# Branch prefetch hints on four engines, the fp64 weights decoded in the expert units, their clamp on GpSimd

## The chip, the cores and the metric

The kernel runs on one core of a Trainium2 chip. The metric is the device time in microseconds (us) of one execution; several executions are timed, and their median counts. One further execution is recorded by the hardware profiler, and all rows below come from that one. Engines: PE = TensorE, DVE = VectorE, ACT = ScalarE, POOL = GpSimd, SP = SyncE (it issues most DMAs).

## The reference

Three layers follow one another on 2304 tokens with 512 channels, in float32; the weights of the third are given as float64.

```
x = decayed_causal_attention(q, k, v, f)        # 4 x 8 heads, 576 tokens, 64 wide
e = argmax(x @ w_gate + bias[modality])          # 8 experts, top 1
x = p[e] * (relu(x @ w1[e]) @ w2[e])             # 512 -> 1024 -> 512
gate = sigmoid(x @ moe2_w_gate)                  # 512 -> 1536, float64 weights
out = (gate * (x @ moe2_w_val)) @ moe2_w_out     # 1536 -> 512, float64 weights
```

## The kernel before

The program has three stages, one behind the other.

**Attention and routing** take the first 240 us or so. The routing sorts the tokens by expert.

**Expert units** (class `Experts`). A unit is 256 sorted tokens of one expert (units 0 to 8, `NA` = 9, method `pair`) or 128 (units 9 and up, `single`). Units 0 and 1 run beside the attention; units 2 to 8 stand behind it and take 23.46 us each, in eight steps f = 0 to 7. In a step PE multiplies the tokens with a block of w1 (`up`, L1208, 12 matmuls of 128x256) and the step before's activations with a block of w2 (`down`, L1218, 6 matmuls of 128x512). Each float32 operand is split in a high and a low part, so each product is three matmuls: ACT makes the high parts (weights L1125, activations L1178), DVE the low ones (weights `wl` L1131, activations `hl` L1179, tokens `xl` L1165). At the end of each step `extra(u, f)` adds work of the next stage. POOL issues the indirect DMAs that gather a unit's tokens (L1081) and scatter its results (L1188). Units 9 and 10 always run. Units 11 to 17 stand in nested `tc.If(nb > u - NA)` (L1802), where `nb` is read from the routing; with these inputs the first test skips all of them, so each engine takes one branch over the code of seven units.

**Gated layer** (class `Gated`). Three sets of 768 tokens, s = 0 to 2, are multiplied with gate, value (L1543) and output weights (L1631). The chip has no float64, so the float64 weights are turned into float32 on the way: they arrive as pairs of 32-bit words in 36 pieces of 512 KB (`load`, into three buffers `raw`), and `decode` makes a float32 piece of each with integer operations: ACT takes the absolute value of the high words (L1395), DVE clamps it (L1376), shifts it left by three and masks it (L1377), then merges in sign and top bit (L1386) and the upper bits of the low word (L1387). Two finished pieces are written to DRAM (`wd`, L1382) and read back as `wf` and `wof`.

`decode((0,))` issues the clamp and the shift. `decode((1,))` issues, in this order, the DMA of a finished pair, L1386 and L1387 of the piece under work, ACT's L1395 of the next piece and the DMA of a later one. A piece's load is thus issued two calls of `decode((1,))` before ACT reads it, and it waits until L1387 has freed its buffer. Before, `extra` calls one half in every step of units 2 to 8, so four pieces per unit; `AHEAD` = 28 pieces are meant for the expert units, and the last 8, with what is in flight, are decoded in the first set of the gated layer. The trace shows 25 pieces finished by DVE before 454.5 us and 11 after it. Each engine works through its instructions in the order of the program.

Of the kernel before, what the change touches and what calls it, by code (L numbers as in the profile page):

```python
# [10 lines left out]
F32 = mybir.dt.float32  # L11
# [4 lines left out]
ALU = mybir.AluOpType  # L16
# [17 lines left out]
NA = NT // 256  # L34
# [1288 lines left out]
class Gated:  # L1323
# [8 lines left out]
    NB, NH = 768, 384  # L1332
    NP, NS = FF2 // 256, NT // 768

    DIRECT, AHEAD = 4, 28

    STEPS = (0, 0), (1, 1), (4, 2), (3, 3), (5, 4), (6, 5), (2, 6)

# [30 lines left out]
    def decode(self, halves=(0, 1)):  # L1369

        nc = self.nc
        if self.c and 0 in halves:
            o, r = self.c[0][:2]
            nc.vector.tensor_scalar(o.bitcast(F32), o.bitcast(F32), MINH, MAXH, ALU.max, ALU.min)  # L1376
            nc.vector.tensor_scalar(o, o, 3, 0x3FFFFFF8, ALU.logical_shift_left, ALU.bitwise_and)  # L1377
        if 1 not in halves:
            return
        if self.done:  # L1380
            key, t = self.done.popleft()
            nc.sync.dma_start(self.wd[key], t.bitcast(F32))  # L1382
        if self.c:
            o, r, key, part = self.c.popleft()
            hw, lw = r[:, :, 1], r[:, :, 0]
            nc.vector.scalar_tensor_tensor(o, hw, -0x40000000, o, ALU.bitwise_and, ALU.bitwise_or)  # L1386
            nc.vector.scalar_tensor_tensor(o, lw, 29, o, ALU.logical_shift_right, ALU.bitwise_or)  # L1387
            if part:
                self.done.append((key, self.dec.pop(key)))
        if self.r and (len(self.r) > 1 or not self.todo):  # L1390
            key, part, r = self.r.popleft()
            if key not in self.dec:
                self.dec[key] = self.bp.tile([P, 2, 512], I32, tag="dec", name="dec", bufs=3)
            o = self.dec[key][:, part, :]
            nc.scalar.activation(o.bitcast(F32), r[:, :, 1].bitcast(F32), AF.Abs)  # L1395
            self.c.append((o, r, key, part))
        if self.todo:
            key, part = self.todo.popleft()
            self.r.append((key, part, self.load(key, part)))
# [331 lines left out]
MINH = float(_np0.array([0x38000000], dtype=_np0.uint32).view(_np0.float32)[0])  # L1731
MAXH = float(_np0.array([0x47EFFFFF], dtype=_np0.uint32).view(_np0.float32)[0])


@with_exitstack
def decayed_attention_top1_moe_gated_kernel(
    ctx: ExitStack,
    tc: tile.TileContext,
    q, k, v, f, moe_modality_id, moe_w_gate, moe_modality_bias, moe_w1, moe_w2,
    moe2_w_gate, moe2_w_val, moe2_w_out, out,  # L1740
):
    nc = tc.nc
    keep = ctx.enter_context(tc.tile_pool(name="keep", bufs=1))
    dram = ctx.enter_context(tc.tile_pool(name="dram", bufs=1, space=DRAM))
    xd = dram.tile([NT, DX], F32, tag="xd", name="xd")
    yd = nc.dram_tensor("rows_by_expert", [NT, DX], F32, kind="Internal").ap()
    ident = keep.tile([P, P], F32, tag="ident", name="ident")
    make_identity(nc, ident)

    c2 = ExitStack()  # L1750
    ps = Banks(c2.enter_context(tc.tile_pool(name="ps", bufs=1, space=PSUM)))
    raw = c2.enter_context(tc.tile_pool(name="ex_r", bufs=1))
    with ExitStack() as c1:
        ro = Routing(tc, c1, keep, xd, ident, moe_modality_id, moe_w_gate, moe_modality_bias)
        ex = Experts(tc, ro, ps, raw, xd, yd, moe_w1, moe_w2)
        ex.g[0], ex.g[1] = ro.xg[0:2], ro.xg[2:4]
        with ExitStack() as c0:
            with ExitStack() as top:
                with tc.manual_schedule():
                    att = Attention(tc, c0, top, ro, ps, q, k, v, f)  # L1760
                    ex.begin(att)
                    att.run(ex)
            ro_t = c1.enter_context(tc.tile_pool(name="ro_t", bufs=1, side="right", reuse_waits="tile"))
            with tc.manual_schedule():
                ex.tail(ro.finish(ro_t, ps), c1.enter_context(tc.tile_pool(name="ex_s", bufs=1, side="right", reuse_waits="tile")))
        sp = c2.enter_context(tc.tile_pool(name="sp", bufs=2, reuse_waits="tile"))
        ex.open(c2, sp)
        ctx.enter_context(tc.manual_schedule())
        ex.rest()

    bits = ctx.enter_context(tc.tile_pool(name="bits", bufs=1, side="right", reuse_waits="tile"))
    ga = Gated(tc, ro, bits, dram, ps, yd, moe2_w_gate, moe2_w_val, moe2_w_out, out)
    none = lambda u, f: None
    with c2:

        pace, todo = (1, 1, 1, 1, 1, 1, 1, 1), deque((0, 1) * (len(ga.todo) + 3))
        turns, first = deque((n, c) for n in range(2) for c in range(KD)), deque()

        def extra(u, f):
            if u < NA:  # L1780
                for _ in range(min(pace[f], len(todo))):
                    ga.decode((todo.popleft(),))

            if u == NA - 2 and f == 4:
                ga.rows(0)
            if u == NA - 1 and f == 4:
                ga.tokens(0)
            if u == NA - 1 and f >= 4 or u >= NA and f in (0, 4):
                ga.early(*turns.popleft())
            if u == NA + 1 and f == 0:  # L1790
                ga.fetch(0)
            if u == NA + 1 and f == 3:
                first.extend(f for _, f in ga.prepare(0))
            if u == NA + 1 and f == 5:
                ga.fetch(1)
            if u == NA + 1 and f >= 5:
                for _ in range(min(2, len(first))):
                    first.popleft()()

        ex.run(range(2, NA + 2), NA + 1, extra)  # L1800
        nb = nc.values_load(ro.tl[0:1, 2 * NU:2 * NU + 1], min_val=0, max_val=NB)
        with ExitStack() as ifs:  # L1802
            for u in range(NA + 2, NU):
                ifs.enter_context(tc.If(nb > u - NA))
                ex.start(u)
                ex.run([u], u, none)

    with ExitStack() as c3:
        ga.run(c3)
# [33 lines left out]
```

## Time and profile before

| what | us |
|---|---|
| timed runs | 905.07, 905.3, 906.23 (median 905.3) |
| profiled execution | 906.16 |
| its span, first to last instruction | 904.2 |
| PE busy | 871.4 (96%) |
| DVE busy | 691.4 (76%) |
| ACT busy | 547.4 (61%) |
| POOL busy | 233.1 (26%) |

All times of rows are counted from the span's start. The expert units end at 454.5 us, the gated layer begins at 458.0 us. A "busy" share is a mean over stages: between 300 and 420 us DVE is at 93%, at the end of the program far below that.

### The profile page before, as it was taken

To read this page: it belongs to the slowest core of one execution; us is meant where nothing else is said; L and a number is where in the kernel's file an instruction comes from. 1 tells how busy PE (TensorE), PEld (TensorE's weight loads), DVE (VectorE), ACT (ScalarE), POOL (GpSimd) and SP (SyncE) were. 2 spreads that over 40 slices of the span, in tenths; PEclk is the share of its full clock that TensorE was granted. 3 is DMA by queue.
4 is the path that set the end of the run, shared out by engine and by line. 5 is a ranking of instruction groups with operands and counts; after the bars stand their busy time and mean duration, and the time that the engine had idled before them with its cause. 6 is when DMAs were issued, how large, how long until landed. Compare 5 with 4: busy or idle time off the path is not lost. (4 is left out here: it accounts for less than half of the span.)

```text
span 904.2 us, 16679 instructions
## 1 busy us (share of the span) xinstructions
PE 871.4 (96%) x5563; PEld 757.2 (84%) x5563; DVE 691.4 (76%) x1665; ACT 547.4 (61%) x1179; POOL 233.1 (26%) x483
## 2 busy tenths in 40 slices
PE   8998999979999999999989899999999999999996
PEld 6776777758989999999779888999988999999995
DVE  7677788848888999999767886887665888766652
ACT  7776777754456666667834545566555567545442
POOL 5787777674542222111000000002000001100002
PEclk9999999999999999999989999999999999999999
DMA  6555666786535955589766423244221212312201
GB/s 147 131 124 140 173 162 147 217 211 162 100 106 166 331 180 178 184 240 341 254 236 191 140 70 94 71 141 140 70 71 51 89 61 96 104 67 70 70 1 70
DMA packets 121133, 126.54 MB, mean 140 GB/s; under 512 B 68208, under 2 KB 95344, under 8 KB 121040
## 3 DMA queue, kind: packets, MB, share of 16 engines
q1 hardware_dynamic: 115744, 110.48, 42.6%
q0 software_dynamic: 4640, 14.70, 4.8%
q8 instruction: 46, 0.75, 0.4%
q14 instruction: 47, 0.39, 0.1%
q10 hardware_dynamic: 656, 0.22, 0.1%
HBM read 126.78 MB, written 24.28 MB: 167 GB/s over the span
## 5 line engine op out<-in xcount | busy, mean ns | idle before, releaser
L1543 PE MATMUL g<-x,wc 128*128 128x384 f32 x1536 | 304.4, 340 | 10.6 <-PEq L1802 3.5
L1543 PEld LDWEIGHTS g<-x,wc 128*128 128x128 f32 x1536 | 275.9, 189 | 31.0 <-ACT pc L1580 4.4
L1631 PE MATMUL o<-wo,ah 128*128 128x512 f32 x648 | 184.5, 397 | 0.2 <-DVE ah L1568 0.2
L1631 PEld LDWEIGHTS o<-wo,ah 128*128 128x128 f32 x648 | 118.0, 188 | 11.7 <-DVE ah L1568 1.0
L1639 POOL DMA_INDIRECT out_dram<-os,tok x18 | 18.4, 1020 | 423.7 <-ACT os L1638 418.2
L1567 ACT ACTIVATE ah<-s 128x384 fp32r<-128x384 f32 x72 | 37.9, 526 | 99.9 <-DVE s L1566 96.6
L1131 DVE TENSOR_TENSOR wl<-ws,wh 128x1024 fp32r<-128x1024 f32 x76 | 92.3, 1217 | 1.0 <-ACT wh L1125 1.0
L1125 ACT ACTIVATE wh<-ws 128x1024 fp32r<-128x1024 f32 x76 | 80.4, 1062 | 15.6 <-PE y L1218 15.6
L293 POOL TENSOR_SCALAR dec<-cum 128x192 f32<-128x192 f32 (+4 forms) x150 | 79.9, 539 | 25.6 <-DMA cum<-drow 16.5
L360 ACT ACTIVATE sc<-sc,mn 128x192 f32<-128x192 f32 (+2 forms) x144 | 82.3, 573 | 2.9 <-DVE mn L352 2.4
L352 DVE CUSTOM_DVE_ANT_0 sc<-s,dec 128x192 f32<-128x192 f32 (+2 forms) x144 | 58.7, 441 | 22.5 <-POOL dec L293 8.7
L1208 PE MATMUL h<-xh,wh 128*128 128x256 f32 x240 | 69.0, 288 | 0.0
L1208 PE MATMUL h<-xl,wh 128*128 128x256 f32 x240 | 67.7, 282 | 0.0
L1208 PE MATMUL h<-xh,wl 128*128 128x256 f32 x240 | 67.7, 282 | 0.0
L1580 ACT ACTIVATE pc<-g 128x384 f32<-128x384 f32 x96 | 46.3, 483 | 31.1 <-PE g L1543 30.6
L1188 POOL DMA_INDIRECT rows_by_expert<-ys,dst x18 | 22.1, 1229 | 159.0 <-ACT ys L1187 56.4
L345 PE MATMUL s<-qk,qT 64*128 64x320 f32 (+4 forms) x384 | 55.7, 407 | 3.7 <-DVE mn L352 2.2
L1426 DVE TENSOR_TENSOR wc<-wf,wc 128x512 fp32r<-128x512 f32 x72 | 40.7, 568 | 18.2 <-ACT wc L1423 18.2
L1559 ACT ACTIVATE sg<-sg 128x384 f32<-128x384 f32 x48 | 25.2, 525 | 45.3 <-DVE sg L1589 18.8
L345 PEld LDWEIGHTS s<-qk,qT 64*128 64x128 f32 (+1 forms) x384 | 31.2, 177 | 23.6 <-issue 16.3
L1218 PE MATMUL y<-wh,hh 128*128 128x512 f32 x120 | 47.6, 397 | 0.7 <-ACT hh L1178 0.7
L1218 PE MATMUL y<-wh,hl 128*128 128x512 f32 x120 | 47.3, 394 | 0.6 <-DVE hl L1179 0.6
(306 smaller groups left out, 1809.5 us busy)
## 6 DMA issues: line engine op xcount, KB each, us to landing
ws<-in_moe_w_dram SPq DMA_DIRECT2D x88, 512.0 KB
wf<-wd SPq DMA_DIRECT2D x36, 512.0 KB
wd<-dec SPq DMA_DIRECT2D x18, 512.0 KB
wof<-wd SPq DMA_DIRECT2D x18, 512.0 KB
cum<-drow SPq DMA_DIRECT2D x30, 288.0 KB
raw<-in_moe_w_gate_dram SPq DMA_DIRECT2D x12, 512.0 KB
raw<-in_moe_w_val_dram SPq DMA_DIRECT2D x12, 512.0 KB
raw<-in_moe_w_out_dram SPq DMA_DIRECT2D x12, 512.0 KB
```

The costliest lines, as they stand in the source:

```text
L293: nc.gpsimd.tensor_scalar(d[r, o], c[r, z], -1.0, c[r, a:a + 1], ALU.mult, ALU.add)
L345: nc.tensor.matmul(out[r, o:o + w], q[a, rows], k[a, c:c + w], start=True, stop=True)
L352: nc.vector.tensor_tensor_reduce(s[:, so + c0:so + e], t[j, b, c0][:, 0:e - c0], d[:, do + c0:do + e], -1.0, mn[j][:, 5:6] if c0 else 3.0e ...
L360: nc.scalar.activation(so, so, AF.Exp, bias=mn[j][:, b:b + 1], scale=-1.0, accum_out=sm[:, c:c + 1])
L1125: self.nc.scalar.activation(hi, self.ws[k], AF.Copy)
L1131: eng.tensor_tensor(lo, self.ws[k], hi.bitcast(F32), ALU.subtract)
L1208: nc.tensor.matmul(t, a[:, c, cs], self.chunk(b, c), start=(n == 0), stop=(n == 3 * KD - 1))
L1218: nc.tensor.matmul(y[j], a[:, cs], b[:, f % 2, :], start=(f == 0 and n == 0), stop=(f == nf - 1 and n == 2))
L1426: V(t["w"][:, 1, to], of(), t["w"][:, 0, to].bitcast(F32), ALU.subtract)
L1543: self.nc.tensor.matmul(t, p[:, c, :], q[:, c, :], start=(first and n == 0), stop=(n == total - 1), skip_group_check=not first)
L1580: nc.scalar.activation(c, t, AF.Copy)
L1631: nc.tensor.matmul(o[0], x[:, cs], y[:, r, :], start=(o[1] == 0 and k == 0), stop=(o[1] == 2 * self.NP - 1 and k == 2))
```

## The change

`AHEAD` becomes 36: every piece is decoded in the expert units. The clamp goes from DVE to POOL (same operation and tile), the shift moves to the other half, ahead of the two merges. The one-half-per-step pace is replaced by a table of steps per unit, `slots`: in each of them the second half of one piece and the first half of the next are issued. That is five pieces in each of units 3 to 8, two in unit 9 and one in unit 10; all 36 loads are issued by the end of unit 8. A branch hint, "likely taken", is set for PE, ACT, DVE and SP on the first of the nested tests; POOL has none.

```diff
-    DIRECT, AHEAD = 4, 28
+    DIRECT, AHEAD = 4, 36
...
         if self.c and 0 in halves:
             o, r = self.c[0][:2]
-            nc.vector.tensor_scalar(o.bitcast(F32), o.bitcast(F32), MINH, MAXH, ALU.max, ALU.min)
-            nc.vector.tensor_scalar(o, o, 3, 0x3FFFFFF8, ALU.logical_shift_left, ALU.bitwise_and)
+            nc.gpsimd.tensor_scalar(o.bitcast(F32), o.bitcast(F32), MINH, MAXH, ALU.max, ALU.min)
...
             hw, lw = r[:, :, 1], r[:, :, 0]
+            nc.vector.tensor_scalar(o, o, 3, 0x3FFFFFF8, ALU.logical_shift_left, ALU.bitwise_and)
             nc.vector.scalar_tensor_tensor(o, hw, -0x40000000, o, ALU.bitwise_and, ALU.bitwise_or)
...
-        pace, todo = (1, 1, 1, 1, 1, 1, 1, 1), deque((0, 1) * (len(ga.todo) + 3))
+        slots = {2: (2, 3, 5, 6, 7), **dict.fromkeys(range(3, NA), (0, 2, 3, 6, 7)), NA: (1, 4), NA + 1: (1,)}
...
-            if u < NA:
-                for _ in range(min(pace[f], len(todo))):
-                    ga.decode((todo.popleft(),))
+            if (u, f) == (2, 0):
+                ga.decode((1,))
+                ga.decode((1,))
+            if f in slots.get(u, ()):
+                ga.decode((1,))
+                ga.decode((0,))
...
             if u == NA + 1 and f == 0:
+                tc.mark_branch_hint_location("more", "LikelyTaken", [e.engine for e in (nc.tensor, nc.scalar, nc.vector, nc.sync)])
                 ga.fetch(0)
...
-                ifs.enter_context(tc.If(nb > u - NA))
+                ifs.enter_context(tc.If(nb > u - NA, label="more" if u == NA + 2 else None))
```

Four lines are added above the branch, so L1802 of before is L1806 of the change; L1376 is the clamp in both; the shift L1377 is L1385 of the change, and L1386 and L1387 keep their numbers.

In the built program the hint stands not beside the branch but at the start. PE, start of the program:

```order
-L1838 UNCONDITIONAL_BRANCH
+L1842 UNCONDITIONAL_BRANCH
+L1842 BRANCH_PREFETCH_HINT
 L132 MATMUL t<-x 128x128 x10
```

The branch that it speaks of comes some 1,880 lines of this listing later; ACT, DVE and SP have it at the same place.

DVE, one stretch of steps in the middle of the expert units. `hl` and `wl` are the low parts that PE needs in the next steps, `dec` is a piece under work, `raw` its float64 words. Before:

```order
L1179 SCALAR_TENSOR_TENSOR hl<-h,hh 128x256
L1131 TENSOR_TENSOR wl<-ws_104,wh 128x1024
L1376 TENSOR_SCALAR dec<-dec 128x512
L1377 TENSOR_SCALAR dec<-dec 128x512
L1179 SCALAR_TENSOR_TENSOR hl<-h,hh 128x256
L1131 TENSOR_TENSOR wl<-ws_105,wh 128x1024
L1386 SCALAR_TENSOR_TENSOR dec<-raw,dec 128x512
L1387 SCALAR_TENSOR_TENSOR dec<-raw,dec 128x512
```

and with the change:

```order
L1179 SCALAR_TENSOR_TENSOR hl<-h,hh 128x256
L1131 TENSOR_TENSOR wl<-ws_104,wh 128x1024
L1385 TENSOR_SCALAR dec<-dec 128x512
L1386 SCALAR_TENSOR_TENSOR dec<-raw,dec 128x512
L1387 SCALAR_TENSOR_TENSOR dec<-raw,dec 128x512
L1179 SCALAR_TENSOR_TENSOR hl<-h,hh 128x256
L1131 TENSOR_TENSOR wl<-ws_105,wh 128x1024
L1179 SCALAR_TENSOR_TENSOR hl<-h,hh 128x256
```

The clamp has left DVE; the three operations of a piece stand in one block, and five steps of eight have one.

POOL, the same units. Before it had only indirect DMAs:

```order
L1081 DMA xg<-xd,ids 128x513 x2
L1188 DMA rows_by_expert<-ys,dst 2304x513 x2
L1081 DMA xg<-xd,ids 128x513 x2
L1188 DMA rows_by_expert<-ys,dst 2304x513 x2
L1081 DMA xg<-xd,ids 128x513 x2
```

and with the change:

```order
L1376 TENSOR_SCALAR dec<-dec 128x512 x3
L1081 DMA xg<-xd,ids 128x513 x2
L1376 TENSOR_SCALAR dec<-dec 128x512 x2
L1188 DMA rows_by_expert<-ys,dst 2304x513 x2
L1376 TENSOR_SCALAR dec<-dec 128x512 x3
```

Three clamps now stand ahead of each unit's gather, and two ahead of its scatter.

## Rows read from the trace of the kernel before

**Rows 1.** Stretches of time, us: length, busy time (instructions), PE clock, DMA share, GB/s.
```profile
core 0: us, PE busy (x) PEld busy (x) DVE busy (x) ACT busy (x) POOL busy (x), PEclk, DMA share, GB/s
...
325.00:350.00 25.00, 25.00 (x162) 22.54 (x161) 23.24 (x43) 16.54 (x26) 5.22 (x4) 1.00 0.53 170
...
400.00:420.00 20.00, 20.00 (x134) 18.16 (x134) 18.60 (x39) 13.80 (x24) 4.22 (x3) 1.00 0.95 312
...
440.00:454.50 14.50, 13.97 (x87) 11.48 (x86) 11.29 (x17) 10.53 (x20) 1.22 (x1) 1.00 0.40 152
454.50:458.00 3.50, 0.02 (x1) 0.00 (x0) 2.28 (x5) 0.69 (x1) 0.97 (x1) 0.77 0.12 36
458.00:462.00 4.00, 3.96 (x12) 3.99 (x13) 0.00 (x0) 0.00 (x0) 0.00 (x0) 0.50 0.64 154
...
500.00:520.00 20.00, 17.69 (x93) 15.77 (x93) 17.45 (x38) 11.24 (x24) 0.00 (x0) 1.00 0.51 158
520.00:540.00 20.00, 18.25 (x97) 16.26 (x96) 16.46 (x39) 9.58 (x21) 0.00 (x0) 1.00 0.27 79
540.00:560.00 20.00, 18.23 (x100) 16.29 (x99) 13.29 (x29) 10.35 (x23) 0.00 (x0) 1.00 0.35 106
...
650.00:700.00 50.00, 48.82 (x263) 44.61 (x262) 31.15 (x69) 26.82 (x56) 0.00 (x0) 1.00 0.18 53
```

**Rows 2.** Waits of the gated layer: engine, line, releaser: us, times, longest.
```profile
PE g L1543 <- PEq L1802: 3.5, 1, 3.5
```

**Rows 3.** Line 1802, the branch, by engine queue: duration in ns, start in us.
```profile
L1802 PEldq COMPARE_BRANCH  x1: 3792/3792/3792, 453.9 to 453.9; - x1
...
L1802 ACTq COMPARE_BRANCH  x1: 54/54/54, 455.1 to 455.1; - x1
...
L1802 ACTq EVENT_SEMAPHORE  x1: 17/17/17, 458.0 to 458.0; - x1
```

**Rows 4.** Chain that ended last: start us, us, what.
```profile
458.04 8.88 PE g L1543 x36
...
481.48 2.09 PE g L1543 x12
```

**Rows 5.** Stretches of time, instructions on tile `dec` alone: DVE, ACT, POOL.
```profile
277.00:454.50 177.50, 55.65 (x100) 17.47 (x26) 0.00 (x0) 1.00 0.70 231
454.50:560.00 105.50, 24.48 (x44) 6.66 (x10) 0.00 (x0) 0.97 0.50 157
```

**Rows 6.** Tile `dec`, DVE's operations on a piece: ns min/median/max.
```profile
L1376 DVE TENSOR_SCALAR dec<-dec x36: 416/421/428, 279.9 to 537.7; 128x512 f32<-128x512 f32 x36
L1377 DVE TENSOR_SCALAR dec<-dec x36: 426/428/429, 280.4 to 538.2; 128x512 int32<-128x512 int32 x36
L1386 DVE SCALAR_TENSOR_TENSOR dec<-raw,dec x36: 681/686/693, 282.8 to 538.6; 128x512 int32<-128x512 int32 x36
L1387 DVE SCALAR_TENSOR_TENSOR dec<-raw,dec x36: 691/692/695, 283.5 to 539.4; 128x512 int32<-128x512 int32 x36
```

**Rows 7.** Timeline of POOL, the scatter of two units: start us, us, what.
```profile
332.30 1.01 POOL L1188 DMA_INDIRECT rows_by_expert<-ys,dst  x1 [17.33 <-DVE ys L1186]
...
355.76 1.02 POOL L1188 DMA_INDIRECT rows_by_expert<-ys,dst  x1 [17.33 <-DVE ys L1186]
```

**Rows 8.** Groups of POOL by form: busy us, mean ns | idle before.
```profile
L293 POOL TENSOR_SCALAR dec<-cum 128x576 f32<-128x576 f32 x30 | 22.0, 745 | 0.0
L293 POOL TENSOR_SCALAR dec<-cum 128x448 f32<-128x448 f32 x30 | 19.0, 643 | 1.5
```

**Rows 9.** Timelines of POOL and DVE, routing: start us, us, what.
```profile
209.69 2.39 POOL L1131 TENSOR_TENSOR spare<-ws,spare 128x1024 fp32r<-128x1024 f32 x1
...
210.41 1.70 DVE L420 TENSOR_SCALAR r<-sm 128x9 f32<-128x9 f32 x1
```

**Rows 10.** One raw piece, its load on SP and ACT's reading; landing of the gathers.
```profile
408.03 0.38 SPq L1361 DMA_DIRECT2D raw<-in_moe_w_gate_dram  x1
...
418.03 0.69 ACT L1395 ACTIVATE dec<-raw 128x512 f32<-128x512 f32 x1 [0.82 <-DMA raw<-in_moe_w_gate_dram]
...
DMA to landing us min/median/max: 4.4/5.9/7.2
```

## The prediction

> **What bounds the kernel now.** I read the stretches of time first, since the busy shares of the whole program hide which engine limits which stage. In the expert units PE is busy without a gap and DVE nearly so: 23.24 us of 25.00, 93%, while ACT has a third of its time free and POOL four fifths [rows 1]. PE sets the pace there and DVE stands just under it. The second thing to see is the seam at 454.5 us: for 3.50 us PE does nothing, and in the four microseconds behind it PE's granted clock is 0.50, the lower of its two levels [rows 1]. The waits name the releaser: PE's own sequencer, at the branch of L1802, 3.5 us [rows 2]; the branch itself took 3792 ns on PE from 453.9 us, and ACT, whose branch took 54 ns at 455.1, has its next event at 458.0 [rows 3]. The chain that ended last starts there too: its first 36 matmuls took 8.88 us, while 12 at full clock take 2.09 [rows 4]. Third, behind 500 us PE loses 2.31, 1.75 and 1.77 us in three stretches of 20 us, against 1.18 in 50 us later on [rows 1]; the first two of them still hold decoding, of which 24.48 us on DVE and 6.66 us on ACT lie behind the branch [rows 5].
>
> **The change, part by part.**
>
> *Branch hint.* If it does what its name says, PE finds its code behind the branch ready. PE's idle time of 3.5 us [rows 2] would go, but for some 0.2 us for the branch itself (54 ns on ACT) and the semaphores beside it [rows 3]: about 3.3. With no pause the clock need not fall either: 36 matmuls at the full pace of rows 4 take 3 x 2.09 = 6.27, so 8.88 - 6.27 = 2.6 us come back. Sum -5.9. Bounds: 0 if the hint does nothing, -6.1 if nothing at all is left; what is late next is ACT, whose branch and events end at 458.0 [rows 3] and which has a hint too. I take -5.9, being nearer the row that shows the whole wait at one instruction. The hint instruction itself stands at the start of the program; I bound it by 0 and the 0.05 us of ACT's branch [rows 3] and take 0.
>
> *Gated layer.* It no longer decodes 11 pieces. PE's idle time between 500 and 560 us is 2.31 + 1.75 + 1.77 = 5.83 us. At the later rate (1.18 in 50, so 0.47 in 20) the first two stretches would give 4.06 - 0.94 = 3.1 us. The third has no decoding after 539.4 [rows 6] and loses as much as the second, so part of the idle time is not DVE's decoding but something else, perhaps weights read back late; of it I count 0.4. I take -3.5; bounds 0 (it is all something else) and -5.8 (all goes).
>
> *Expert units 3 to 8, DVE.* A unit lasts 355.76 - 332.30 = 23.46 us [rows 7]; DVE is busy 0.93 x 23.46 = 21.8 and idle 1.64. Four pieces cost 4 x (421 + 428 + 686 + 692) ns = 8.91 us; five without their clamp cost 5 x 1.806 = 9.03 [rows 6]. That alone is +0.12 and harmless. The clamp on POOL is not shown; between 448 and 576 columns POOL's tensor_scalar takes 643 to 745 ns [rows 8], so some 0.69 us for 512. POOL has room for five of them. The doubt is whether DVE stands still meanwhile. One place shows that it can: POOL's L1131 ran from 209.69 to 212.08, and a tiny DVE operation of 9 columns, begun at 210.41, ended at 212.11, 0.03 us behind it [rows 9]. So each clamp may hold DVE for anything between 0 and 0.69 us. Some of it lies beside DVE work that is not held or beside a wait, so I take 0.45. Then DVE needs 21.8 + 0.12 + 5 x 0.45 = 24.2 us in a unit of 23.46: 0.75 too much, and over six units +4.5 us, since PE can then only wait for `hl` and `wl`. Bounds: 0 (clamps in DVE's idle time) to 6 x (0.12 + 5 x 0.69 - 1.64) = +11.6.
>
> The Trainium skill ("SBUF — State Buffer", section "SBUF: two separate sides") speaks against this move: DVE and GpSimd share a pair of ports, and the one that starts first holds it for its whole instruction while the other is blocked. Rows 9 agree with it in that one place. By that rule a clamp that has started would hold back the merges and `wl`, and the sum would go towards the upper bound; a clamp that arrives during them would wait at no cost to DVE.
>
> *Raw loads.* A load is issued when L1387 frees its buffer, and read by ACT two calls later. Before, that is always four steps, 11.73 us, of which 10.00 - 0.82 = 9.2 were left in the case of rows 10. With the table of steps the distance is two steps from f = 6 to the next f = 0 (3.3 us left), three from 0 to 3 and from 7 to 2 (6.2 left), four otherwise. Landing takes 4.4 to 7.2 us for the gathers, which are half as large, and 10 us for a raw piece where the DMA engines are 95% busy [rows 1, 10]. So ACT will wait 1 to 4 us in every unit, 2 or so of which its third of free time takes, and more where expert weights are loaded as well. Bounds 0 and +8 (two such units of the six, one wait of 3.8 us each unhidden, doubled); I take +1.0, nearer 0, since ACT waited only 0.82 us in the fullest stretch so far. POOL's gathers stand behind three clamps now, that is some three steps (9 us) later, but a unit ahead of their use; the scatter's two clamps are short. Both I price at nothing: a whole unit of 23.46 us covers them.
>
> *Units 9 and 10.* They decode three pieces more, 5.4 us on DVE. DVE has 14.50 - 11.29 = 3.2 us free in 440 to 454.5, and PE loses 0.53 there already [rows 1]. I take +1.0; bounds 0 and +3.
>
> Sum: -5.9 - 3.5 + 4.5 + 1.0 + 1.0 = -2.9. The profiled execution took 906.16 us (its span 904.2 and 1.96 around it), so it would take 903.3. It lies 0.86 above the median of the timed runs, 905.3, and against the median the forecast is **902.4 us**.
>
> **Rivals.** 0.2% of the time, 1.8 us, is about what a measurement of this kernel can tell from no change: below 903.5 is faster, above 907.1 slower.
>
> *A. The hint does nothing* (it stands 450 us ahead of its branch, and may be forgotten by then). For: its place in the built program. Against: it names the branch. PE's wait and its low clock stay, the other terms as they are: 902.4 + 5.9 = **908.3**, slower. It makes the kernel slower once the other four terms are above +1.8; by my sum they are +3.0. Should the clamps be harmless too, 903.8. The Trainium skill ("Runtime: NRT & Kernel Launch", section "Instruction fetch mechanics") says that instructions are fetched ahead only in sequence and that a taken branch out of that window waits for its target's page. The 3792 ns of PE's branch agree with that; on what a hint does the section is silent.
>
> *B. DVE becomes the bound.* Each clamp holds DVE for its full 0.69 us: the third term is +11.6 and not +4.5. Then all gains are lost: -5.9 - 3.5 + 11.6 + 1.0 + 1.0 = +4.2, **909.5**, slower. It decides once a clamp holds DVE for more than 0.61 us on average: then the third term is 6 x (0.12 + 3.05 - 1.64) = +9.2 and the sum passes +1.8. For: DVE's merges and `wl` fill most of each step, so that a clamp seldom meets a free DVE. Against: the clamp waits for ACT's L1395 and then for whatever DVE is at, and `hl` may run beside it.
>
> *C. The clamps cost nothing.* They fall in DVE's 1.64 us of idle time or beside operations that are not held. Third term 0: 902.4 - 4.5 = **897.9**; with a little more from the gated layer 896. For: only 3.45 us of clamps per unit, and a hold of under 0.30 us each fits into the idle time. Against: rows 9.
>
> **How the numbers follow.** Forecast 0.40 (hint works, DVE slightly over; 0.28 of it faster, 0.11 within 1.8 us, 0.01 slower); A 0.22 (0.02 faster, 0.06 the same, 0.14 slower); B 0.17 (0.01 the same, 0.16 slower); C 0.18, all faster; 0.03 for raw loads that land later than I think, half of it the same and half slower. Together: faster 0.48, the same 0.20, slower 0.32. The range reaches to C below and A and half of B above: 896 to 910. Within the likeliest case alone it is 899 to 906.
>
> **What would show it.** In the new profile: PE's branch under 0.3 us and the granted clock 1.00 behind it, the first 36 matmuls of L1543 in about 6.3 us; if the branch still takes 3.8 us, A holds. The distance of two scatters in the middle units: 23.46 says C, 24.2 the forecast, 25 and more B; DVE's L1131, L1385 and L1386 longer than before, beside POOL's L1376, would show the hold. No instruction on `dec` behind the branch, and PE's idle time between 500 and 560 us down by 3 to 4 us. ACT's waits for `raw` at the first step of each unit. I am wrong if the gated layer's idle time stays as it is (then it was not DVE that caused it), or if the units slow down for another reason than DVE.

## The result and the profile after

The changed kernel takes 911.78 us (median of 5 runs, 909.62 to 914.67), the kernel before 905.3 (5 runs). The ratio is 1.0075 with a 95% interval of 1.0046 to 1.0103: **slower by 6.5 us**, and outside the predicted range, which ended at 910. The profiled execution took 914.67 us (span 913.0): it is the slowest of the five, 2.9 us above their median, so the stages below add up to 8.8 us and not to 6.5.

The stretches of time, as in [rows 1], of the changed kernel (length, then busy time of PE, PE's weight loads, DVE, ACT and POOL, PE's clock, DMA share, GB/s):

```profile
325.00:350.00 25.00, 24.66 (x156) 21.25 (x155) 24.36 (x40) 16.33 (x26) 16.64 (x10) 1.00 0.61 193
...
440.00:460.00 20.00, 16.83 (x88) 13.78 (x87) 16.46 (x25) 12.28 (x23) 5.26 (x4) 0.83 0.92 320
470.00:480.00 10.00, 9.45 (x50) 8.22 (x50) 2.18 (x5) 3.12 (x5) 0.98 (x1) 1.00 0.36 120
480.00:500.00 20.00, 18.14 (x97) 16.68 (x97) 11.60 (x22) 8.56 (x18) 0.00 (x0) 1.00 0.46 158
500.00:520.00 20.00, 20.00 (x107) 18.81 (x106) 13.14 (x28) 9.47 (x22) 0.00 (x0) 1.00 0.17 57
520.00:540.00 20.00, 19.29 (x103) 16.99 (x102) 12.11 (x31) 10.52 (x23) 0.00 (x0) 1.00 0.22 76
540.00:560.00 20.00, 20.00 (x110) 18.36 (x109) 12.27 (x25) 10.31 (x22) 0.00 (x0) 1.00 0.26 79
```

DVE is at 97% in the middle units now, and PE is no longer without gaps there. Between 440 and 460 us (unit 9) PE loses 3.2 us and its clock falls to a mean of 0.83. After 500 us PE is nearly full: the gated layer gained. The branch and the wait behind it, which answer to [rows 2, 3]:

```profile
L1806 PEldq COMPARE_BRANCH  x1: 392/392/392, 471.6 to 471.6; - x1
```
```profile
PE g L1543 <- PEq L1806: 0.4, 1, 0.4
```

The branch takes 0.39 us instead of 3.79. The decoding operations, as in [rows 6], with the clamp on POOL:

```profile
L1376 POOL TENSOR_SCALAR dec<-dec x36: 1907/2266/2907, 268.6 to 443.6; 128x512 f32<-128x512 f32 x36
L1385 DVE TENSOR_SCALAR dec<-dec x36: 417/502/855, 270.6 to 453.9; 128x512 int32<-128x512 int32 x36
L1386 DVE SCALAR_TENSOR_TENSOR dec<-raw,dec x36: 691/693/1016, 271.4 to 454.3; 128x512 int32<-128x512 int32 x36
L1387 DVE SCALAR_TENSOR_TENSOR dec<-raw,dec x36: 691/692/1292, 272.2 to 455.0; 128x512 int32<-128x512 int32 x36
```

A clamp takes POOL 2.27 us, not the 0.69 that the rows of another operation on POOL suggested, and DVE's operations have a tail: the shift takes up to 0.86 us, twice its time of before. The waits between 277 and 470 us show two things that were hardly there before:

```profile
PEld y L1218 <- DVE hl L1179: 11.5, 21, 2.0
...
ACT dec L1395 <- DMA raw<-in_moe_w_gate_dram: 7.4, 2, 6.7
ACT dec L1395 <- DMA raw<-in_moe_w_val_dram: 6.5, 4, 4.7
ACT dec L1395 <- DMA raw<-in_moe_w_out_dram: 4.5, 5, 2.2
```

PE's weight loads wait 21 times for DVE's low parts, 11.5 us (before: once, 1.0), and ACT waits 18.4 us for raw pieces (before: 2.3).

**Where the time went.** PE executes the same matmuls in the same order in all kernels of this study, so the start of one and the same matmul can be compared between two traces, and the growth of the difference from one point to the next is what a stage lost (+) or gained (-). The points are the first matmul of `up` in units 2, 3, 4, 8 and the first of L1248 in unit 9 (before: 258.19, 283.47, 306.92, 400.76 and 425.10 us), the last of L1264 in unit 10 (454.13), and of L1543 the 193rd (503.00, in the gated layer) and the last (887.37). In us, against the kernel before; the runs are explained below. What a kernel differs already ahead of unit 2 (from -1.7 to +4.2 us) lies in the attention and routing, whose program no run edits, and is left out.

| run | unit 2 | unit 3 | units 4 to 7 | unit 8 | units 9, 10 | seam to 503 us | gated layer |
|---|---|---|---|---|---|---|---|
| the changed kernel | +1.80 | +3.74 | +4.71 | +2.03 | +5.56 | -3.33 | -5.54 |
| e1, hint alone | 0.0 | 0.0 | 0.0 | 0.0 | 0.0 | -2.02 | +0.35 |
| e2, without hint | +1.82 | +5.15 | +4.86 | +3.37 | +5.56 | -0.97 | -5.27 |
| e3, clamp on DVE | +1.60 | +7.95 | +2.12 | +4.52 | +4.33 | -4.82 | -5.56 |
| e4, no clamp | +0.91 | +7.61 | 0.0 | +4.14 | +3.97 | -2.71 | -5.54 |
| f2, none in 9, 10 | +1.81 | +6.15 | +5.01 | +2.14 | +0.13 | +2.93 | -5.57 |
| f3, hint, old pace, clamp on POOL | 0.0 | +1.14 | +2.78 | +0.69 | 0.0 | +3.12 | -0.31 |
| f5, four in 3 and 8 | +1.82 | 0.0 | +4.87 | 0.0 | 0.0 | +3.55 | -3.96 |
| f6, the same, clamp on DVE | +1.62 | +0.13 | +3.16 | 0.0 | 0.0 | -1.63 | -3.95 |
| g1, f5, gated clamp on DVE | +1.58 | 0.0 | +5.05 | 0.0 | 0.0 | -3.24 | -3.93 |
| g2, hint and a little more | 0.0 | 0.0 | +1.82 | 0.0 | +3.62 | -2.80 | -1.60 |
| g3, f6 with bunched loads | +1.61 | +10.99 | +2.00 | +8.43 | 0.0 | -3.57 | -3.93 |
| g4, hint on PE alone | 0.0 | 0.0 | 0.0 | +0.34 | +0.06 | -2.11 | +0.39 |

So the changed kernel gains 3.3 us at the seam and 5.5 us in the gated layer, and loses 17.8 us in the expert units ahead of them. Units 3 and 8 scatter most: e2 and f2 have the same program there as the changed kernel and lose 8.5 and 8.3 us in the two together, against 5.8. Three losses of different kinds can be seen in its trace.

*Unit 3.* SP, then ACT, then PE, in their timelines:

```profile
292.24 0.44 SPq L1361 DMA_DIRECT2D raw<-in_moe_w_gate_dram  x1
293.03 1.18 SPq L1098 DMA_DIRECT2D ws<-in_moe_w_dram  x2
```
```profile
301.80 0.66 ACT L1395 ACTIVATE dec<-raw 128x512 f32<-128x512 f32 x1 [6.68 <-DMA raw<-in_moe_w_gate_dram]
302.36 0.37 ACT L1178 ACTIVATE hh<-h 128x256 fp32r<-128x256 f32 x1
```
```profile
302.79 0.50 PE L1218 MATMUL y<-wh,hh 128*128 128x512 f32 x1 [2.59 <-ACT hh L1178]
```

A raw load issued at 292.24 is read at 301.80, while the weights of the next expert are loaded; ACT stands 6.68 us, the activations `hh` stand behind it in ACT's order, and PE stands 2.59 us behind those. ACT was ready to read at 301.80 - 6.68 = 295.12, only 2.9 us after the load's issue, and the piece took 9.6 us to arrive. In units 4 to 7 ACT reads some pieces 4.2 us after their issue, and waits 1.2 us at most.

*The middle units.* Timelines of POOL and of DVE around two clamps:

```profile
343.34 4.72 POOL L1376 TENSOR_SCALAR dec<-dec 128x512 f32<-128x512 f32 x2
348.81 2.91 POOL L1376 TENSOR_SCALAR dec<-dec 128x512 f32<-128x512 f32 x1 [0.76 <-ACT dec L1395]
```
```profile
342.71 1.67 DVE L1131 TENSOR_TENSOR wl<-ws,wh 128x1024 fp32r<-128x1024 f32 x1
...
349.86 0.83 DVE L1385 TENSOR_SCALAR dec<-dec 128x512 int32<-128x512 int32 x1
350.73 0.69 DVE L1386 SCALAR_TENSOR_TENSOR dec<-raw,dec 128x512 int32<-128x512 int32 x1
...
352.40 1.22 DVE L1131 TENSOR_TENSOR wl<-ws,wh 128x1024 fp32r<-128x1024 f32 x1
```

The `wl` that runs when a clamp starts takes 1.67 us instead of 1.22, the shift beside a clamp 0.83 instead of 0.42; L1386 in the middle of the same clamp takes its usual 0.69. It isn't the same operation each time: L1387 takes 0.98 us beside some clamps, and L1386 1.02 beside the one of unit 9. Over units 4 to 7 DVE's operations take 7.6 us more than their usual times, for 20 clamps. So some 0.4 us of DVE's time go with a clamp, about what the clamp itself took on DVE (0.42). By the rule of the Trainium skill ("SBUF — State Buffer", section "SBUF: two separate sides"), a DVE operation with two inputs in SBUF, as L1386 is, would be blocked while a clamp that started first still runs. Here L1386 began 1.9 us into the clamp of 348.81, ended before it, and took its usual time; these rows do not agree with the rule.

*Unit 9.* PE, in its timeline:

```profile
443.01 0.50 PE L1264 MATMUL y<-wh,hh 128*128 128x512 f32 x1 [0.84 <-ACT hh L1178]
...
445.53 0.80 PE L1264 MATMUL y<-wh,hl 128*128 128x512 f32 x1 [1.79 <-DVE hl L1179]
```
```profile
443.00:447.00 4.00, 2.20 (x6) 1.48 (x7) 3.54 (x5) 1.18 (x2) 2.90 (x2) 0.72 1.05 367
447.00:451.00 4.00, 4.00 (x19) 3.80 (x18) 1.56 (x2) 1.70 (x3) 0.00 (x0) 0.50 1.01 316
```

A piece's three operations on DVE, two of them slowed beside a clamp, stand ahead of the `hl` that PE needs; PE pauses, and its granted clock then is at the lower level for the 4 us of the second row. The slowing beside a clamp is the smaller part of it: in the table e3 and e4, which have no clamp on POOL, lose 4.33 and 3.97 us in units 9 and 10.

### The profile page after: what moved, and what is told of

Read it like the earlier page. It is cut to its first block, busy times and chain, and to the rows that moved or that the text cites. A ratio compares the mean times of both kernels' runs of the same rounds, so it can differ in the third digit from the quotient of the medians.

```text
span 913.0 us, 16711 instructions
## 1 busy us (share of the span) xinstructions
PE 875.6 (96%) x5563; PEld 754.4 (83%) x5563; DVE 691.1 (76%) x1629; ACT 546.8 (60%) x1179; POOL 315.6 (35%) x519
## 4 chain that ended last, share of the span: by engine, by line
PE 45%; issue 19%; DVE 13%; DMA 10%; POOL 7%; ACT 2%; SPq 1%; POOLq 0%; DVEq 0%; ACTq 0%
PE g L1543 18%; PE o L1631 10%; DMA rows_by_expert<-ys,dst 4%; PE h L1208 4%; DVE wl L1131 4%; PE y L1218 3%; PE s L345 2%; POOL dec L293 2%; PE t L379 2%; PE o L436 2%; DVE dec L1386 2%; POOL dec L281 2%; DMA raw<-in_moe_w_val_dram 1%; DVE dec L1385 1%; DVE hl L1179 1%
## 5 line engine op out<-in xcount | busy, mean ns | idle before, releaser
L1543 PE MATMUL g<-x,wc 128*128 128x384 f32 x1536 | 301.4, 338 | 4.7 <-ACT pc L1580 2.3
L1543 PEld LDWEIGHTS g<-x,wc 128*128 128x128 f32 x1536 | 273.6, 188 | 24.3 <-ACT pc L1580 3.6
L1376 POOL TENSOR_SCALAR dec<-dec 128x512 f32<-128x512 f32 x36 | 82.1, 2286 | 49.1 <-ACT dec L1395 49.0
L1131 DVE TENSOR_TENSOR wl<-ws,wh 128x1024 fp32r<-128x1024 f32 x76 | 95.8, 1263 | 1.0 <-ACT wh L1125 1.0
```

Source lines behind the costliest of these rows:

```text
L1131: eng.tensor_tensor(lo, self.ws[k], hi.bitcast(F32), ALU.subtract)
L1376: nc.gpsimd.tensor_scalar(o.bitcast(F32), o.bitcast(F32), MINH, MAXH, ALU.max, ALU.min)
L1543: self.nc.tensor.matmul(t, p[:, c, :], q[:, c, :], start=(first and n == 0), stop=(n == total - 1), skip_group_check=not first)
```

## The experiments

The kernel before was timed again beside each group of runs (medians 907.82 us for e1 to e4, 904.08 for the runs f, 909.2 for the runs g), and each ratio is to the one beside it.

**e1: the hint alone.** The kernel before with the two lines of the hint.

```diff
+                tc.mark_branch_hint_location("more", "LikelyTaken", [e.engine for e in (nc.tensor, nc.scalar, nc.vector, nc.sync)])
...
+                ifs.enter_context(tc.If(nb > u - NA, label="more" if u == NA + 2 else None))
```

> The kernel before with the branch hint alone. Theory (the hint acts, the decoding is what made the change slow): PE's branch falls from 3.79 to about 0.4 us, as in the changed kernel, and the clock behind it stays up: 3.4 us, with the clock 6.0, less than 905.3, so 899.3 to 901.9. Rival (the short branch of the changed kernel came from other instructions standing in memory, not from the hint): branch still near 3.8 us and 905.3.

Measured: ratio 0.9978 (0.9962 to 0.9994), so 2.0 us less; the branch takes 0.39 us. The theory of the hint holds, the size does not: the gated layer starts 3.2 us earlier, but 1.2 us of them are given back before 503 us. The stretches, the waits and ACT's timeline behind the branch:

```profile
458.00:462.00 4.00, 4.00 (x25) 3.86 (x24) 1.77 (x4) 3.03 (x5) 0.00 (x0) 1.00 0.74 266
462.00:466.00 4.00, 2.18 (x13) 1.86 (x13) 1.52 (x3) 1.71 (x4) 0.00 (x0) 1.00 0.17 23
466.00:470.00 4.00, 4.00 (x15) 4.00 (x16) 3.88 (x9) 1.24 (x3) 0.00 (x0) 0.57 1.09 305
```
```profile
PE g L1543 <- ACT sg L1559: 1.8, 1, 1.8
```
```profile
464.29 1.15 ACT L1423 ACTIVATE wc<-wf 128x512 fp32r<-128x512 f32 x2 [3.25 <-DMA rows_by_expert<-ys,dst]
```

What is late next is the scatter of the last unit: ACT waits 3.25 us for it before it may write `wc`, PE pauses 1.8 us behind ACT, and the low clock, gone behind the branch, comes 8 us later (0.57). In the changed kernel ACT waits for the same scatter and PE 1.24 us behind it:

```profile
472.53 8.66 PE L1543 MATMUL g<-x,wc 128*128 128x384 f32 x48 [0.36 <-PEq L1806]
482.43 4.50 PE L1543 MATMUL g<-x,wc 128*128 128x384 f32 x24 [1.24 <-ACT sg L1559]
```
```profile
480.86 1.15 ACT L1423 ACTIVATE wc<-wf 128x512 fp32r<-128x512 f32 x2 [3.39 <-DMA rows_by_expert<-ys,dst]
```

**e2: the changed kernel without the hint.**

```diff
-                tc.mark_branch_hint_location("more", "LikelyTaken", [e.engine for e in (nc.tensor, nc.scalar, nc.vector, nc.sync)])
...
-                ifs.enter_context(tc.If(nb > u - NA, label="more" if u == NA + 2 else None))
+                ifs.enter_context(tc.If(nb > u - NA))
```

> The changed kernel without the hint. Theory: the branch is back at about 3.8 us, so 3.4 to 6 us above 911.8: 915.2 to 917.8. Rival (the hint does nothing): 911.8 and a branch of 0.4 us.

Measured: ratio 1.0131 (1.0105 to 1.0157), against 1.0075 with the hint. The branch is back:

```profile
L1805 PEldq COMPARE_BRANCH  x1: 4032/4032/4032, 475.2 to 475.2; - x1
```

The hint acts. At the seam it is worth 2.4 us in these two traces (-0.97 against -3.33); the rest of the difference lies in units 3 and 8, where raw loads come late by different amounts from run to run.

**e3: the clamp back on DVE; e4: no clamp.**

```diff
-            nc.gpsimd.tensor_scalar(o.bitcast(F32), o.bitcast(F32), MINH, MAXH, ALU.max, ALU.min)
+            nc.vector.tensor_scalar(o.bitcast(F32), o.bitcast(F32), MINH, MAXH, ALU.max, ALU.min)
```

For e4 the line is left out.

> The changed kernel with the clamp back on DVE, everything else as changed. Theory A (five pieces are too much for DVE, and the clamp on GpSimd takes from DVE's other operations the 0.41 us that it saves): no clear difference, 910 to 913, DVE operations back at 0.43, 0.69 and 1.22 us. Rival B (the contention with GpSimd is the cause): about 5 to 12 us less, 900 to 907. Rival C (the uneven distances of the raw loads are the cause): 911 to 913 and the same long waits of ACT for raw pieces.

> The changed kernel without any clamp (a part of the computation left out: weights outside the range of float32 would come out wrong), so five pieces cost DVE 9.03 us a unit and GpSimd nothing. Theory A: the middle units are back at 23.46 us, some 7 us less; the waits for raw pieces in units 3, 8 and 9 stay: 903 to 906. Rival C (the raw loads alone): the middle units stay near 24.6 us, 909 to 912.

Measured: e3 1.0107 (1.0086 to 1.0127), e4 1.0066 (1.0050 to 1.0082). Both totals lie above theory A's, and both theories were half right; the table by stage tells them apart. In units 4 to 7 five pieces cost nothing without a clamp (0.0), 0.53 us a unit with it on DVE (2.12 in four) and 1.18 with it on POOL (4.71). The stretch of 331 to 378 us, in this order, of the kernel before, of e4, whose units take 23.46 us again, of e3, of the changed kernel and of f3 (below):

```profile
331.00:378.00 47.00, 47.00 (x307) 42.53 (x306) 43.56 (x79) 31.59 (x49) 10.42 (x8) 1.00 0.56 183
331.00:378.00 47.00, 47.00 (x306) 42.53 (x305) 44.56 (x77) 32.75 (x52) 11.60 (x8) 1.00 0.68 217
331.00:378.00 47.00, 46.90 (x301) 41.31 (x300) 46.28 (x86) 31.73 (x50) 11.16 (x8) 1.00 0.64 207
331.00:378.00 47.00, 46.16 (x288) 39.72 (x287) 45.71 (x73) 31.94 (x49) 34.81 (x18) 1.00 0.63 205
331.00:378.00 47.00, 46.13 (x300) 41.23 (x300) 41.82 (x70) 30.38 (x47) 24.09 (x16) 1.00 0.53 178
```

So in the middle units DVE's work on the pieces is the cause, with the clamp as the part that is too much, and moving it to POOL made it worse by 0.65 us a unit, not better. That is not DVE's sum: DVE, the third busy time of a row, is busy longer in e3 (46.28 us) than in the changed kernel (45.71), and e3 loses less. What grows is PE's wait for low parts: over units 4 to 7 its weight loads wait 8 times, 3.5 us, for `hl` in e3 and 12 times, 6.8 us, in the changed kernel. But units 3 and 8 lose 7.61 and 4.14 us even without any clamp: there something else is the cause, and the raw loads (Rival C) fit it: ACT's longest waits for raw pieces in e4 are 8.2 and 6.9 us, and PE waits 4.5 and 2.9 us for the `hh` behind them. The run g3 below tests this by itself.

**f2: no decoding in units 9 and 10.**

```diff
-        slots = {2: (2, 3, 5, 6, 7), **dict.fromkeys(range(3, NA), (0, 2, 3, 6, 7)), NA: (1, 4), NA + 1: (1,)}
+        slots = {2: (2, 3, 5, 6, 7), **dict.fromkeys(range(3, NA), (0, 2, 3, 6, 7)), }
```

> The changed kernel with no decoding in units 9 and 10; the three pieces that were decoded there are decoded in the gated layer. Theory (in unit 9 the decoding stands ahead of the low parts that PE waits for, and the pause lowers PE's clock): the 5.5 us that PE loses in unit 9 go, the gated layer takes some 1.5 us back, so about 4 us less than the changed kernel, ratio to before 1.003. Rival (unit 9 is late because the expert weights arrive late, whatever is decoded): unit 9 still loses 4 us or more, ratio 1.007.

Measured: ratio 1.0099 (1.0070 to 1.0127). The loss of units 9 and 10 went from 5.56 to 0.13 us, as the theory says, and yet the kernel was not faster: the seam lost 2.93 us where it had gained 3.33. There DVE waits 11.0 us for POOL's first clamp of the gated layer, and POOL 7.1 us for the last scatter; the next run has the same wait.

**f3: the hint and the old pace, the clamp on POOL.** From e1:

```diff
-            nc.vector.tensor_scalar(o.bitcast(F32), o.bitcast(F32), MINH, MAXH, ALU.max, ALU.min)
-            nc.vector.tensor_scalar(o, o, 3, 0x3FFFFFF8, ALU.logical_shift_left, ALU.bitwise_and)
+            nc.gpsimd.tensor_scalar(o.bitcast(F32), o.bitcast(F32), MINH, MAXH, ALU.max, ALU.min)
...
+            nc.vector.tensor_scalar(o, o, 3, 0x3FFFFFF8, ALU.logical_shift_left, ALU.bitwise_and)
             nc.vector.scalar_tensor_tensor(o, hw, -0x40000000, o, ALU.bitwise_and, ALU.bitwise_or)
```

> The hint, the old even pace of four pieces a unit and 28 pieces, but the clamp on GpSimd and the shift in the second half. Theory A (the clamp takes from DVE's neighbours what it frees): DVE's time for a unit is the same within 0.5 us, the units stay at 23.46 us and the time is that of the hint alone, ratio 0.998. Rival B (GpSimd's contention by itself slows the units): middle units of 24 us and more, ratio 1.000 to 1.004.

Measured: ratio 1.0083 (1.0060 to 1.0107), against 0.9978 for e1: the clamp on POOL, with the shift moved behind it, costs 1%. Its middle units take 24.16 us, as Rival B said, and theory A is wrong; but contention is not the main cause. In the middle units (0.70 us each) DVE waits for the clamp, which is queued on POOL behind the scatter and another clamp: 1.82 us, once a unit, ahead of the `hl` that PE then waits for. The shift behind that wait takes some 0.4 us more than usual, and DVE has less to do in all (41.82 us of 47 against 43.56 before, in the rows above). In the gated layer it waits much longer. DVE in a middle unit and at the seam, POOL and PE at the seam:

```profile
338.42 0.83 DVE L1385 TENSOR_SCALAR dec<-dec 128x512 int32<-128x512 int32 x1 [1.82 <-POOL dec L1376]
```
```profile
467.56 0.83 DVE L1385 TENSOR_SCALAR dec<-dec 128x512 int32<-128x512 int32 x1 [9.15 <-POOL dec L1376]
```
```profile
465.61 6.01 POOL L1376 TENSOR_SCALAR dec<-dec 128x512 f32<-128x512 f32 x3 [5.24 <-DMA rows_by_expert<-ys,dst]
```
```profile
472.71 1.65 PE L1543 MATMUL g<-x,wc 128*128 128x384 f32 x4 [4.82 <-DVE wc L1426]
```

POOL waits for the last unit's scatter before it goes on to the gated layer's clamps; DVE waits 9.15 us for the first of them, the `wc` behind it come late, and PE stands 4.82 us. The changed kernel avoids this only because it has no piece left to decode by then.

**f5 and f6: four evenly spaced pieces in units 3 and 8, none in 9 and 10.** f5 has the clamp on POOL, f6 on DVE.

```diff
-        slots = {2: (2, 3, 5, 6, 7), **dict.fromkeys(range(3, NA), (0, 2, 3, 6, 7)), NA: (1, 4), NA + 1: (1,)}
+        slots = {2: (2, 3, 5, 6, 7), **dict.fromkeys(range(4, NA - 1), (0, 2, 3, 6, 7)), 3: (1, 3, 5, 7), NA - 1: (1, 3, 5, 7)}
...
-        nset, spare, rests = 2 * self.NP, deque([0, 1] * (len(self.late) + 4)), []
+        nset, spare, rests = 2 * self.NP, deque([0, 1] * (len(self.late) + 6)), []
```

> The changed kernel with four evenly spaced pieces in units 3 and 8, in which expert weights are loaded, five in units 4 to 7, none in units 9 and 10; five pieces are left to the gated layer. Theory (raw loads that come late are the larger loss): ACT's long waits for raw pieces go and with them the losses of units 3, 8 and 9, some 11 us; the quiet units keep their 1.2 us each; the gated layer takes back 2.5; so 8 us less than the changed kernel, ratio 0.999. Rival (five pieces and GpSimd's contention are all): losses in units 3 and 8 of 1.2 us each remain, ratio 1.003 or more.

> As the run with four pieces in units 3 and 8, with the clamp on DVE. In the earlier run with the clamp on DVE the middle units lost 0.53 us each where the clamp on GpSimd lost 1.2. Theory: four such units, so 2.5 us less than with the clamp on GpSimd, ratio 0.996. Rival A (both places cost the same): the same ratio as with GpSimd.

Measured: f5 1.0068 (1.0041 to 1.0095), f6 1.0002 (0.9986 to 1.0018). In both the losses of units 3, 8, 9 and 10 are gone, as the theory said. f5's total missed its expectation by the same seam as f2 and f3 (+3.55); f6, which has no clamp on POOL, has the seam at -1.63, and lies 6.0 us below f5, but missed its 0.996, which was reckoned from f5's own expectation. The middle units cost 3.16 us with the clamp on DVE and 4.87 on POOL.

**g1: f5 with the gated layer's clamps on DVE.**

```diff
-            nc.gpsimd.tensor_scalar(o.bitcast(F32), o.bitcast(F32), MINH, MAXH, ALU.max, ALU.min)
+            (nc.gpsimd if self.lp is None else nc.vector).tensor_scalar(o.bitcast(F32), o.bitcast(F32), MINH, MAXH, ALU.max, ALU.min)
```

> As the run with four pieces in units 3 and 8 and the clamp on GpSimd, but in the gated layer the clamp is on DVE. Theory (GpSimd's clamp there stands behind its wait for the last scatter, DVE behind the clamp and PE behind DVE): the 6 us that PE lost at the seam go, ratio 1.0015 instead of 1.0068; the quiet units keep their 1.2 us each. Rival (the seam is late for another reason): PE still loses 4 us or more there, ratio above 1.005.

Measured: ratio 0.9997 (0.9981 to 1.0014); the seam is at -3.24 instead of +3.55. The explanation of the seam holds.

**g3: f6 with the four pieces of units 3 and 8 in steps 0 to 3.**

```diff
-        slots = {2: (2, 3, 5, 6, 7), **dict.fromkeys(range(4, NA - 1), (0, 2, 3, 6, 7)), 3: (1, 3, 5, 7), NA - 1: (1, 3, 5, 7)}
+        slots = {2: (2, 3, 5, 6, 7), **dict.fromkeys(range(4, NA - 1), (0, 2, 3, 6, 7)), 3: (0, 1, 2, 3), NA - 1: (0, 1, 2, 3)}
```

> As the run with four pieces in units 3 and 8 and the clamp on DVE, but those four pieces in steps 0 to 3 instead of 1, 3, 5 and 7, so that a raw load has two steps instead of four until ACT reads it. Theory (the distance of the raw loads is what hurts where expert weights are loaded): ACT waits 4 us and more for single raw pieces, PE loses 3 us or more in unit 3 and 2 or more in unit 8, where the even order lost nothing; ratio 1.005. Rival (the fifth piece was the cause): no loss in units 3 and 8, ratio 1.000.

Measured: ratio 1.0192 (1.0171 to 1.0213). With the same number of pieces, unit 3 loses 10.99 us and unit 8 8.43, where even spacing lost 0.13 and nothing. ACT, then PE, in unit 3:

```profile
307.29 0.66 ACT L1395 ACTIVATE dec<-raw 128x512 f32<-128x512 f32 x1 [10.27 <-DMA raw<-in_moe_w_gate_dram]
```
```profile
308.27 0.80 PE L1218 MATMUL y<-wh,hh 128*128 128x512 f32 x1 [7.09 <-ACT hh L1178]
```

Steps 0 to 3 also bunch DVE's work, but in unit 3 PE's weight loads wait only 1.4 us for `hl`, against 7.3 for the `hh` behind the raw piece; behind the pause the granted clock is at the lower level for 4 us (0.50 from 308 to 312 us). The distance between a raw load and its use is what hurts most where expert weights are loaded, not the fifth piece.

**g2: the hint, the clamp on DVE, and three pieces more.** From e1: one half more in each of units 4 to 7, one piece in unit 10.

```diff
-    DIRECT, AHEAD = 4, 28
+    DIRECT, AHEAD = 4, 31
...
-                for _ in range(min(pace[f], len(todo))):
+                for _ in range(min(pace[f] + (f == 2 and 4 <= u < NA - 1), len(todo))):
...
+            if (u, f) == (NA + 1, 1):
+                ga.decode((todo.popleft(),))
+                ga.decode((todo.popleft(),))
```

> The hint and the old pace with the clamp on DVE, with one half piece more in each of units 4 to 7, into DVE's idle 1.64 us (half a piece takes 1.11), and one piece in unit 10, where the changed kernel lost nothing: three pieces leave the gated layer. Theory (a piece costs nothing as long as DVE's time in a unit stays below 23.46 us, and leaves PE some 0.5 us in the gated layer): units 4 to 7 at 23.46 us and 1.5 us less than the hint alone, ratio 0.996. Rival (any piece more delays the low parts of some step): units at 23.6 or more and ratio 0.998 or above.

Measured: ratio 1.0018 (1.0005 to 1.0030). The rival holds: DVE's idle time of a whole unit does not help when one step gets more than it can hold; the four units lost 1.82 us (PE's weight loads wait four times for `hl` there, 2.5 us), and the piece in unit 10 cost 3.62.

**g4: the hint on PE alone.** From e1:

```diff
-                tc.mark_branch_hint_location("more", "LikelyTaken", [e.engine for e in (nc.tensor, nc.scalar, nc.vector, nc.sync)])
+                tc.mark_branch_hint_location("more", "LikelyTaken", [nc.tensor.engine])
```

> The kernel before with the hint on PE alone. Theory (PE's own branch is the wait): PE's branch 0.4 us and the first matmul of the gated layer as early as with four hints, ratio 0.998. Rival (the other engines' code arrives as late, and PE then waits for ACT or SP): less than half of the gain at the seam, ratio 0.999 to 1.000.

Measured: ratio 0.9968 (0.9953 to 0.9983), not to be told from e1. At its first matmul behind the branch PE has gained less than in e1, since it waits for DVE's branch next:

```profile
PE g L1543 <- DVEq L1803: 1.7, 1, 1.7
```

So the rival had a point: DVE, without a hint, goes on only 2.9 us after its own branch (branch at 455.9 us, next event at 458.8). By 503 us both have gained the same (2.11 and 2.02 us), by two ways: e1 starts 3.2 us earlier and then waits for the scatter, g4 starts 1.8 us earlier, has the low clock at once (0.57 from 459 to 463 us) and no wait for the scatter behind it. e1 and g4 are the versions that beat the kernel before and the changed one.

## Why the prediction was wrong, step by step

The forecast was 902.4 us by a sum of -2.9; the trace's sum is +9.0 (the row of the changed kernel; with the 0.2 that it was early ahead of unit 2, 8.8). **The step that failed** is the price of decoding in the expert units. It was taken from sums, DVE's free time in a unit or a stretch and ACT's one wait so far, where the runs show that what counts is which `hl` or `hh` stands behind a piece. It shows most in units 9 and 10, 5.6 us instead of 1.0 and the one term outside its bounds, and in the raw loads.

- **Branch hint**, predicted -5.9. The whole seam gained 3.3 us, 1.0 of it without the hint as well (e2); the hint itself is worth 2.4 by that comparison and 2.0 in e1. The branch fell from 3.79 to 0.39 us as predicted, so rival A was wrong: a hint at the program's start still acts 450 us and more later. Behind it the granted clock was 1.00, and 48 matmuls took 8.66 us, that is 6.5 for 36, near the 6.3 of the forecast. But the time was given back to the next waits, since the step "what is late next is ACT" named the engine but not the wait: the last unit's scatter, and behind it ACT's `wc`. On the fetch of code the section of the Trainium skill that the prediction cites ("Runtime: NRT & Kernel Launch", "Instruction fetch mechanics") fits what e2 shows, 4.03 us for a taken branch without a hint.
- **Gated layer**, predicted -3.5 with bounds 0 and -5.8, measured -5.5. Nearly all of PE's idle time there went with the decoding after all, in the third stretch too.
- **DVE in the expert units**, predicted +4.5 as 0.75 in each of six units; measured 1.18 in each of units 4 to 7, 24.64 us a unit, between the sign of the forecast (24.2) and that of rival B (25). DVE's busy time came near the forecast: 45.71 of 47 us is 23.96 in such a unit, where 24.2 was predicted, and the hold per clamp was near too (0.45 taken, some 0.4 seen). But only 0.5 of the 1.18 us lies in that sum; for the other 0.7 DVE had idle time, only not ahead of the low parts that PE waited for. The clamp's own duration was mis-sized, 2.27 us instead of 0.69: the rows taken for it were of an operation on GpSimd with a multiplication and an addition, not a maximum and a minimum. And one term was missing: unit 2, where the table puts pieces into three successive steps at its end and PE then waits 1.56 us for `hl`, was priced at nothing and cost 1.8 us.
- **Raw loads**, predicted +1.0 with bounds 0 and 8. Units 3 and 8 cost 5.8 us in this trace; if DVE costs 1.18 in each of them as elsewhere, some 3.4 are left for the raw loads, and some 6 in e2 and f2. "ACT waited only 0.82 us in the fullest stretch so far" was taken as the nearest row, though that row belonged to a distance of four steps, and the same paragraph had worked out 6.2 us for three steps against a landing of 10. In unit 3 even that was too much: over three steps the load of 292.24 had 2.9 us left, since the L1387 that frees its buffer ended only at 290.74 and SP still had weights of the next expert and a `wd` to issue. The bound held, and the value chosen from it was too low. f6 and g3 show the mechanism: 0.13 and 10.99 us in unit 3 with nothing changed but the spacing.
- **Units 9 and 10**, predicted +1.0 with bounds 0 and 3, measured 5.6, outside the bounds. DVE's free time there was summed over the stretch; what decides is that one piece stands ahead of one `hl`. The pause costs twice, as PE's clock falls behind it. f2 shows it: 0.13 without the pieces.
- **POOL's queue**, priced at nothing. In the changed kernel DVE's waits for a clamp stay at 1.6 us in all, and no clamp stands behind the last scatter, but f3 shows how near it was: with pieces left for the gated layer PE waits 4.8 us.

Rival B named the right engine (DVE) for the middle units, with the wrong price, and that its 909.5 us came nearest to the measured time is partly luck: the hint gave less than it assumed, and units 9 and 10 cost more. No rival had the raw loads or units 9 and 10 as its mechanism (0.03 of the chances went to late raw loads), though they cost some 9 of the 17.8 us.

What stays open: how the 0.4 us beside a clamp comes about (a shared port, or something else), and why the clamp on POOL costs PE 0.65 us a unit more than on DVE although DVE is no busier; no run has a clamp on POOL that nobody waits for. Why DVE's own slowing falls on one operation and not on another was not found out either. Nor was a fourth raw buffer tried.

## What to carry to other kernels

Where an engine has idle time in a unit, look at what stands ahead of the next operation that the bounding engine waits for, step by step; the sum over a unit says little on that. When a prefetch is moved, work out its distance in time at each place and compare it with the landing time of the fullest stretch, not of the mean. Work that goes to another engine's queue also takes over everything that this queue waits for; and a gain at a seam is only as large as the time to the next wait behind it.

## What the runs showed of the hardware that was not expected

- The hint instruction stands at the start of the program and acts on a branch 455 to 472 us later: 392 ns on PE instead of 3792 and 4032 without it. With the hint on PE alone the gain in time is the same within the intervals (0.9968 and 0.9978).
- A maximum and minimum over 128x512 float32 takes GpSimd 1.9 to 2.9 us beside DVE's work, where DVE takes 0.42.
- Beside such an operation DVE loses some 0.4 us in all: mostly the shift takes 0.83 us instead of 0.42, while L1386, with two inputs, mostly takes its usual 0.69 (1.02 at the most).
- A raw piece of 512 KB came 9.6 us after its issue while expert weights were loaded too, and 11.8 us in g3; in units 4 to 7, where ACT waited for one, 4.5 to 5.5 us.
